# Moving two elementwise sums of a seven-product tile behind its first bank's reads, and computing six more tiles with seven products

## The chip, the cores and the metric

One core of a Trainium2 chip runs the whole program. The metric is the device time of one execution in microseconds (us). Three runs of the kernel before gave 838.73, 839.22 and 839.88 us, median 839.22 us. One further execution was profiled, and every duration below that carries a row or a place in time comes from it.

## The reference, cut to what matters

```
# x: (8, 3008, 256); w_r, w_i: (256, 256); moe_w_in: (256, 2048); moe_w_out: (2048, 256)
X  = rfft(x, axis=1)
Yr = Xr @ w_r - Xi @ w_i + b_r ;  Yi = Xr @ w_i + Xi @ w_r + b_i
Yr, Yi = soft_threshold(Yr, 0.01), soft_threshold(Yi, 0.01)
y  = irfft(Yr + 1j * Yi, n=3008, axis=1)              # (8, 3008, 256) -> 24064 rows of 256
h  = relu(y @ moe_w_in)                                # 2048 hidden values a row
out = (s * h * h + b) @ moe_w_out                      # 24064 rows of 256
```

The first half (spectral mixing, here "the attention part") is done batch by batch for eight batches. The second half (here "the expert part") takes the 24064 rows in tiles.

## The kernel before, in words

**Tiles and slots.** The rows are cut into 48 tiles, numbered here 0 to 47 in the order in which they are computed; most have 512 rows, some 480 or 384 (`_tile_order`, line 73). A tile takes 16 slots. In each slot `first_mm` (line 851) multiplies one block of 128 hidden units: two matmuls of 512 columns into a double bank `psh`. After every second slot ScalarE (ACT) applies the Relu to the pair (`rt`, line 871, three buffers) and VectorE (DVE) or ACT squares it into `gt` (lines 881 and 884). Which of the two squares is decided while the program is built: the planner adds each instruction's assumed cost to a running sum for each engine and takes the one that is free first (`act_first`, line 180). The second layer of tile t runs in the slots of tile t+1. "The window of tile t" below is that stretch, from the first matmul of tile t+1 to the first of tile t+2. The attention part of a later batch is mixed into the slots by a plan (`schedule`, line 1084). Its matmuls go through one of two `psf` banks, and its evacuations are again split between ACT and DVE. The order in which the instructions stand on each engine is finally set by a scheduling layer; `tc.issue_after(x)` keeps what is issued under it behind x.

**Two ways of doing the second layer.** An ordinary tile (`second_mms`, line 922) multiplies four blocks of 128 rows by 16 blocks of `w_out`: 64 matmuls of 256 columns, four a slot, and two evacuations `ost` (line 945). A tile "by seven products" (`seven_mms`, line 983) uses Strassen's scheme in Winograd's form: the activations and `w_out` are seen as two by two blocks, and seven products of half size take the place of eight. That is 112 matmuls of 128 columns, seven a slot. The right-hand sums (`T_s`) are made once. The left-hand sums are made for each tile and each half q of the hidden units (q is 0 or 1), by `s_op` (line 965), where A11, A12, A21, A22 are parts of `gt`:

- sum 1: s = A21 + A22, on DVE
- sum 3: A21 becomes A11 - A21, on DVE
- sum 2: A11 becomes A11 - s, on DVE, after product 0 has read A11
- sum 4: A12 becomes A12 + A11, as an accumulating DMA that GpSimd (POOL) issues (line 973), after product 1 has read A12

Products 0 and 1 use the old A11 and A12, product 2 uses A22, product 3 uses s, product 4 the new A11, product 5 the new A21, product 6 the new A12. Products 0 and 1 share one PSUM bank, product 2 has the next, products 3 and 4 share the one after, products 5 and 6 the last. In the first seven batches these banks come from the two `psa` buffers, so products 3 and 4 need the bank of products 0 and 1 back. `leave(0)` (line 1020) gives it back: DVE adds product 0 into `zz` (line 1028), product 1 into `ost` (line 1029), and makes a second copy of `zz` (line 1030). `leave(1)` to `leave(3)` take the other products out. In the last batch ("alone" in the code, tiles 41 to 45) the banks rotate over four buffers, and products 0, 1 and 2 are computed together.

**Which tiles, and when.** `seven(ti)` (line 1073) picks 21 tiles: 4 to 6, the two ahead of each batch's first tile from batch 2 on, the first tile of batches 3 to 6 ("late" tiles), and those of the last batch. Batch b's first tile is 12, 17, 23, 29, 35, 41 for b = 2 to 7. For q = 0, sums 1 and 3 are issued in slots 10 and 11 of the tile itself (for late tiles in slots 0 and 1 of its window). All others are issued in its window, at the slots that lines 1061 to 1067 list:

```
*first, (2, 2, 0), (2, 1, 1), (2, 4, 0), (3, 3, 1), (4, 2, 1), (5, 4, 1)     # (slot, sum, q)
...
(4 + alone, 0), (6, 1), (11, 2), (15, 3)                                     # (slot, leave)
```

Queues that matter here: DVE and ACT run their instructions in the order in which they stand. POOL issues the loads of `x` (line 234) and the accumulating DMAs in one order. SyncE (SP) issues the stores of the result and, shortly before a new batch, four loads `us<-ud` of 384 KB each (line 644), which all lie in the window of the tile two ahead of a batch's first.

Of the kernel before, what the change touches and what calls it, by code (L numbers as in the profile page):

```python
# [11 lines left out]
ALU = mybir.AluOpType  # L12
# [84 lines left out]
def kernel(  # L97
# [13 lines left out]
    nc = tc.nc  # L111
    B, S, D = x.shape
# [4 lines left out]
    MC = DFF // P  # L117
# [3 lines left out]
    first, fwd, inv, last = _tables(N)  # L121
# [50 lines left out]
    def matmul(out, lhs, rhs, **how):  # L172
        if pe["on"]:
            pe["now"] += 0.0025 + int(np.prod(rhs.shape[1:])) / 2400.0
        return nc.tensor.matmul(out, lhs, rhs, **how)  # L175

    def work(engine, us):
        load[engine] = max(load[engine], pe["now"]) + us
# [32 lines left out]
    def sum_bank(ti):  # L211
        return any_bank() if ti >= mark[B - 1] // MC else other_bank()
# [149 lines left out]
    b_21 = cpool.tile([P, P], F32, name="b_21")  # L362
# [3 lines left out]
    def w_block(k, j):  # L366
        return w_out_t.rearrange("p (q k) d -> p q k d", k=2)[:, :, k, j * P : (j + 1) * P]
# [447 lines left out]
    def sub_size(tl):  # L815
        return 4 * tl[3] if tl[0] == "wide" else P
# [13 lines left out]
    def halves(ti):  # L830
        return width(tiles[ti]) in (480, 512)
# [54 lines left out]
    def store(tl, sub, src):  # L886
        kind, b, j, w = tl
        if kind == "wide":
            h, lo = j
            n2 = HW * h + 4 * sub  # L890
            rows = out[b * N : (b + 1) * N, :].rearrange("(n1 n2) d -> n2 n1 d", n2=N2)
            nc.sync.dma_start(
                out=rows[n2 : n2 + 4, lo : lo + w], in_=src[0 : 4 * w]
            )
            return
        if kind == "main":
            rows = out[b * N + 512 * j : b * N + 512 * (j + 1), :]
            rows = rows.rearrange("(n1 n2) d -> n2 n1 d", n2=N2)[8 * sub : 8 * sub + 8]
            nc.sync.dma_start(out=rows, in_=src)
            return  # L900
        i0 = j + 128 * sub
        end = min(i0 + 128, j + w)
        i = i0
        while i < end:
            hb, r = divmod(i, N2 * 14)
            n2, n1 = divmod(r, 14)
            bt = 2 * b + hb
            rows = out[bt * N + 80 * N2 : (bt + 1) * N, :].rearrange(
                "(n1 n2) d -> n2 n1 d", n2=N2
            )  # L910
            room = min(end, (hb + 1) * N2 * 14) - i
            if n1 == 0 and room >= 14:
                m = room // 14
                cnt = 14 * m
                dst = rows[n2 : n2 + m]
            else:
                cnt = min(14 - n1, room)
                dst = rows[n2, n1 : n1 + cnt]
            nc.sync.dma_start(out=dst, in_=src[i - i0 : i - i0 + cnt])
            i += cnt  # L920
# [40 lines left out]
    def part(ti, q, i, k):  # L961
        size = 2 * sub_size(tiles[ti])
        return gts[(ti, q)][:, i, k, :, 0:size]

    def s_op(ti, n, q):

        size = 2 * sub_size(tiles[ti])
        if n == 1:
            sums[(ti, q)] = spool.tile([P, 4, 2 * P], F16, name="s1", tag="s1")
        s1 = sums[(ti, q)][:, :, 0:size]  # L970
        a11, a12, a21, a22 = (part(ti, q, i, k) for i in range(2) for k in range(2))
        if n == 4:
            nc.gpsimd.dma_start(out=a12, in_=a11, accum_op=ALU.add)  # L973
            return
        out, a, b, op = {
            1: (s1, a21, a22, ALU.add),
            3: (a21, a11, a21, ALU.subtract),
            2: (a11, a11, s1, ALU.subtract),
        }[n]
        nc.vector.tensor_tensor(out=out, in0=a, in1=b, op=op)  # L980
        work("dve", 0.07 + size / 480.0)

    def seven_mms(ti):

        tl = tiles[ti]
        size = sub_size(tl)
        hold = {}
        left = [(0, 0), (0, 1), (1, 1), None, (0, 0), (1, 0), (0, 1)]
        firsts = (0, 2, 3, 5)
        T = T_s[0]  # L990
        right = [w_block(0, 0), w_block(1, 0), T[:, 3], T[:, 0], T[:, 1], T[:, 2], w_block(1, 1)]

        def mm(n, j, c):

            if n in firsts and j == 0 and c == 0:
                hold["ps"] = sum_bank(ti).rearrange("p (n j e) -> p n j e", n=2, j=2)
            if j == 0 and c == 0:
                hold[n] = hold["ps"][0:size, 0 if n in firsts else 1]
            q, g = divmod(c, 4)
            at = slice(j * size, (j + 1) * size)  # L1000
            if left[n] is None:
                lhs = sums[(ti, q)][:, g, at]
            else:
                lhs = gts[(ti, q)][:, left[n][0], left[n][1], g, at]
            matmul(
                hold[n][:, j], lhs, right[n][:, c],
                start=(n in firsts and j == 0 and c == 0), stop=(c == MC // 2 - 1),
                skip_group_check=True,
            )

        def add(out, of, other):
            nc.vector.scalar_tensor_tensor(  # L1012
                out=out, in0=of, scalar=s_bc[0:size], in1=other, op0=ALU.mult, op1=ALU.add
            )
            work("dve", 0.4)

        def wide(t):
            return t[0:size, 0:P].unsqueeze(1).to_broadcast([size, 2, P])

        def leave(group):  # L1020
            if group == 0:
                hold["z"] = zpool.tile([P, 2, 2, P], F32, name="zz", tag="zz")
            if group in (0, 3):
                hold["o", group] = opool.tile([P, 2, D], F32, name="ost", tag="ost")
            z = hold["z"][0:size]
            top = hold["o", 0][0:size]
            if group == 0:
                add(z[:, 0], hold[0], wide(bias_bc))
                add(top[:, :, 0:P], hold[1], z[:, 0])
                nc.vector.tensor_tensor(out=z[:, 1], in0=z[:, 0], in1=wide(b_21), op=ALU.add)  # L1030
                work("dve", 0.34)
            elif group == 1:
                add(z[:, 0], hold[2], z[:, 0])
            elif group == 2:
                add(z[:, 1], hold[3], z[:, 1])
                two = hold[4].rearrange("p j e -> p (j e)").unsqueeze(1).to_broadcast([size, 2, D])
                zs = z.rearrange("p h j e -> p h (j e)")
                add(zs, two, zs)
                work("dve", 0.27)
            else:  # L1040
                for h in range(2):
                    add(hold["o", 3][0:size, :, h * P : (h + 1) * P], hold[5], z[:, h])
                add(top[:, :, P:D], hold[6], z[:, 1])
                for i in range(2):
                    for j in range(2):
                        store(tl, 2 * (1 - i) + j, hold["o", 3 * (1 - i)][:, j, :])

        C = MC // 2
        alone = ti >= mark[B - 1] // MC
        early = 3 if alone else 2  # L1050
        order = [
            (n, j, c) for h in range(2) for n in range(early) for j in range(2)
            for c in range(4 * h, 4 * h + 4)
        ]
        order += [(n, j, c) for n in range(early, 6) for j in range(2) for c in range(C)]
        order += [(6, j, c) for h in range(2) for j in range(2) for c in range(4 * h, 4 * h + 4)]
        slots = [[] for _ in range(MC)]
        for at, what in enumerate(order):
            slots[at // 7].append(lambda w=what: mm(*w))
        first = ((0, 1, 0), (1, 3, 0)) if late(ti) else ()  # L1060
        for at, n, q in (
            *first, (2, 2, 0), (2, 1, 1), (2, 4, 0), (3, 3, 1), (4, 2, 1), (5, 4, 1)
        ):
            at += alone and at > 3
            slots[at].append(lambda n=n, q=q: s_op(ti, n, q))
        for at, group in ((4 + alone, 0), (6, 1), (11, 2), (15, 3)):
            slots[at].append(lambda group=group: leave(group))
        return slots

    def late(ti):  # L1070
        return any(ti == mark[b] // MC for b in range(3, B - 1))

    def seven(ti):
        if ti >= len(tiles) - 2 or not halves(ti):
            return False
        firsts = [mark[b] // MC for b in range(2, B)]
        return (
            ti >= firsts[-1] or 4 <= ti < 7 or any(m - 2 <= ti < m for m in firsts)
            or late(ti)
        )  # L1080

# [19 lines left out]
    mark = {}  # L1101
# [76 lines left out]
```

## Time and profile before

| what | value |
|---|---|
| three runs | 838.73, 839.22, 839.88 us |
| the profiled execution | 839.64 us, of which the traced span is 837.9 us |
| granted TensorE clock | 0.996 |
| busy DVE, ACT, POOL | 706.9, 723.0, 86.2 us |
| Relu of a pair, 128x1024 | 1026 ns, 328 times |
| square of a pair on DVE / on ACT, 128x1024 | 1221 / 1061 ns |
| one sum on DVE, 128x1024 | about 687 ns |
| accumulating DMA, issue to landing | 3.3 to 8.8 us, median 4.5 us |

Matmuls are pipelined: a matmul's duration holds its way through the array, so the time that a matmul costs is read from the distance between starts, not from its duration. The same goes for DVE to a lesser degree: a 687 ns sum that follows an independent instruction starts 600 ns after it. A tile's window is found in the trace by the first `psh` matmul of each tile; tile 23's, for one, runs from 454.78 to 472.37 us.

### The profile page before, as it was taken

Reading aid. Unit: us, or ns where it says so; the run is one execution under the profiler, and the core shown is the slowest. Engines: PE = TensorE matmul, PEld = TensorE weight load, DVE = VectorE, ACT = ScalarE, POOL = GpSimd, SP = SyncE. Lnnn points to the kernel's source line nnn. Section 1 sums busy time; section 2 is a strip of 40 time slices with the busy share of each in tenths; the row PEclk is TensorE's granted clock in tenths of the full one; section 3 lists DMA queues with packets and bytes.
Section 4 is the critical chain, followed back from the end, with each engine's and each line's share of the span. In section 5 each row is a group of like instructions: output and inputs, shape, how many; then the busy total and the mean of one; then the engine's idle time right before and its main releaser. Section 6 shows DMA issues by size and latency. Waiting matters only on the chain.

```text
span 837.9 us, 19547 instructions
## 1 busy us (share of the span) xinstructions
PE 822.6 (98%) x7662; PEld 600.7 (72%) x7662; DVE 706.9 (84%) x1104; ACT 723.0 (86%) x962; POOL 86.2 (10%) x114
## 2 busy tenths in 40 slices
PE   8999999999999999999999999999999999999997
PEld 7857767777677767777677676767767777767765
DVE  5888989978898888988889888797889988889885
ACT  4998988998899989998889988989889988788882
POOL 4540001100011001100011000100001000001000
PEclk8999999999999999999999999999999999999999
DMA  8954578345873378444773368723565333513321
GB/s 196 180 153 103 124 189 203 63 94 133 198 185 65 94 184 208 114 104 128 195 185 69 88 147 208 175 63 105 127 178 138 67 100 93 137 45 77 72 65 60
DMA packets 116670, 107.17 MB, mean 128 GB/s; under 512 B 12774, under 2 KB 100842, under 8 KB 115234
## 3 DMA queue, kind: packets, MB, share of 16 engines
q1 hardware_dynamic: 102498, 80.55, 33.6%
q0 software_dynamic: 14080, 25.37, 19.1%
q8 instruction: 60, 0.98, 0.5%
q14 instruction: 32, 0.26, 0.1%
HBM read 53.52 MB, written 46.66 MB: 120 GB/s over the span
## 4 chain that ended last, share of the span: by engine, by line
PE 75%; DVE 12%; ACT 6%; DMA 3%; issue 3%; SPq 0%; POOL 0%; DVEq 0%; POOLq 0%
PE psh L175 31%; PE psa L175 28%; PE psf L175 16%; ACT rt L871 3%; DVE gt L884 2%; DVE gt L980 2%; ACT gt L881 1%; DVE ring L699 1%; PE psm L175 1%; DMA gt<-gt 1%; DVE ost L1012 1%; DMA ring<-ring 1%; DVE s L980 1%; DMA x<-in_x_dram 1%; DVE zz L1012 1%
## 5 line engine op out<-in xcount | busy, mean ns | idle before, releaser
L871 ACT ACTIVATE rt<-psh 128x1024 f32<-128x1024 f32 (+2 forms) x384 | 386.7, 1008 | 57.0 <-PE psh L175 55.1
L175 PEld LDWEIGHTS <-gt 128*128 128x128 f16 (+1 forms) x3696 | 304.8, 101 | 167.7 <-DMA gt<-gt 0.5
L175 PE MATMUL psh<-yt,w_in 128*128 128x512 f16 (+1 forms) x1344 | 397.1, 378 | 0.1
L884 DVE TENSOR_TENSOR gt<-rt 128x1024 f16<-128x1024 f32 (+2 forms) x239 | 286.2, 1202 | 78.6 <-ACT rt L871 77.6
L175 PE MATMUL psa<-w_out_t,gt 128*128 128x256 f16 (+3 forms) x2448 | 310.9, 253 | 0.3 <-DMA gt<-gt 0.3
L175 PEld LDWEIGHTS <-w_in 128*128 128x128 f16 x1536 | 136.5, 98 | 24.4 <-issue 1.7
L881 ACT ACTIVATE gt<-rt 128x1024 f16<-128x1024 f32 (+2 forms) x145 | 150.8, 1040 | 3.4
L175 PE MATMUL psa<-T_s,gt 128*128 128x128 f16 (+1 forms) x944 | 79.4, 219 | 0.0
L973 POOL DMA_DIRECT2D gt<-gt x42 | 38.0, 905 | 316.2 <-PE psh L175 66.3
L187 ACT CAST u<-psf 96x512 f16<-96x512 f32 x96 | 55.6, 581 | 9.3 <-PE psf L175 8.6
L699 DVE TENSOR_TENSOR ring<-psf,s 128x512 f16<-128x512 f32 x84 | 57.7, 686 | 3.5 <-PE psf L175 2.5
L187 ACT CAST v<-psf 128x512 f16<-128x512 f32 x79 | 45.8, 583 | 13.6 <-PE psf L175 13.5
L234 POOL DMA_DIRECT2D x<-in_x_dram x36 | 19.2, 539 | 325.1 <-PE psf L175 324.0
L175 PE MATMUL psh<-tail,w_in 128*128 128x512 f16 (+1 forms) x192 | 52.1, 353 | 0.0
L175 PEld LDWEIGHTS <-xf 128*128 128x128 f16 x504 | 46.6, 98 | 6.6 <-DVE xf L672 1.5
L175 PE MATMUL psf<-W_g,xf 128*128 128x256 f16 x336 | 50.4, 272 | 0.0
L187 ACT CAST yt<-psf 128x470 f16<-128x470 f32 (+2 forms) x84 | 43.3, 534 | 3.4 <-PE psf L175 2.2
L1012 DVE SCALAR_TENSOR_TENSOR ost<-psa,s_bc,zz 128x256 f32<-128x256 f32 (+1 forms) x80 | 35.9, 480 | 9.8 <-PE psa L175 8.2
L187 ACT CAST xf<-psf 128x512 f16<-128x512 f32 x64 | 37.4, 585 | 4.2 <-PE psf L175 3.9
L945 DVE SCALAR_TENSOR_TENSOR ost<-psa,s_bc,bias_bc 128x512 f32<-128x512 f32 (+2 forms) x51 | 37.1, 727 | 3.8 <-PE psa L175 1.4
L175 PE MATMUL psf<-x,A_t 94*96 94x512 f16 x102 | 39.0, 382 | 1.4 <-ACT yt L187 0.3
L175 PE MATMUL psf<-C_t,vs 96*128 96x94 f16 (+1 forms) x484 | 37.9, 205 | 0.0
(118 smaller groups left out, 802.6 us busy)
## 6 DMA issues: line engine op xcount, KB each, us to landing
out_dram<-ost SPq DMA_DIRECT2D x152, 128.0 KB
ud<-u SPq DMA_DIRECT2D x56, 192.0 KB
us<-ud SPq DMA_DIRECT2D x28, 384.0 KB
vd<-v SPq DMA_DIRECT2D x42, 256.0 KB
vs<-vd SPq DMA_DIRECT2D x14, 768.0 KB
x<-in_x_dram POOLq DMA_DIRECT2D x28, 376.0 KB, 6.0
gt<-gt POOLq DMA_DIRECT2D x38, 256.0 KB, 4.4
ring<-ring SPq DMA_DIRECT2D x280, 32.0 KB
```

Source lines behind the costliest of these rows:

```text
L175: return nc.tensor.matmul(out, lhs, rhs, **how)
L187: return None, nc.scalar.copy(out=dst, in_=src)
L234: nc.gpsimd.dma_start(out=t[0:N1, i * w : (i + 1) * w], in_=xv[:, c * XCH * D + i * w : c * XCH * D + (i + 1) * w],)
L699: nc.vector.tensor_tensor(out=ring[0][:, i % 4], in0=ps, in1=hold[i // 2][:, i % 2].unsqueeze(1).to_broadcast([P, 2, D]), op=ALU.add,)
L871: nc.scalar.activation(out=rt[:, :, 0:w], in_=ps[:, :, 0:w], func=AF.Relu)
L881: nc.scalar.activation(out=gt, in_=rr, func=AF.Square)
L884: last_square[0] = nc.vector.tensor_tensor(out=gt, in0=rr, in1=rr, op=ALU.mult)
L945: nc.vector.scalar_tensor_tensor(out=ost[0:size, 0:k], in0=ps[0:size, 0:k], scalar=s_bc[0:size], in1=bias_bc[0:size].unsqueeze(1).to_broad ...
L973: nc.gpsimd.dma_start(out=a12, in_=a11, accum_op=ALU.add)
L980: nc.vector.tensor_tensor(out=out, in0=a, in1=b, op=op)
L1012: nc.vector.scalar_tensor_tensor(out=out, in0=of, scalar=s_bc[0:size], in1=other, op0=ALU.mult, op1=ALU.add)
```

## The change

Sums 3 and 2 of half q = 1 now stand behind the third instruction of `leave(0)`; in the list, sum 1 of q = 1 moves from slot 2 to 3, sums 3 and 2 of q = 1 to slot 5, and `leave(0)` is put into its slot ahead of the sums. In the last batch all these are one slot later, as before. The choice of tiles widens from two to three ahead of a batch's first, which adds tiles 9, 14, 20, 26, 32 and 38 (27 tiles by seven products in place of 21). For these six, sum 4 of q = 1 is made by DVE, issued at slot 9, in place of the accumulating DMA.

```diff
+    def third_last(ti):
+        return any(ti == mark[b] // MC - 3 for b in range(2, B))
...
-        if n == 4:
+        if n == 4 and not (q == 1 and third_last(ti)):
             nc.gpsimd.dma_start(out=a12, in_=a11, accum_op=ALU.add)
             return
...
+            4: (a12, a12, a11, ALU.add),
...
-                nc.vector.tensor_tensor(out=z[:, 1], in0=z[:, 0], in1=wide(b_21), op=ALU.add)
+                hold["left"] = nc.vector.tensor_tensor(
+                    out=z[:, 1], in0=z[:, 0], in1=wide(b_21), op=ALU.add
+                )
...
+        def sums_behind(n, q, behind):
+            if behind:
+                with tc.issue_after(hold["left"].ins):
+                    s_op(ti, n, q)
+            else:
+                s_op(ti, n, q)
...
+        slots[4 + alone].append(lambda: leave(0))
         first = ((0, 1, 0), (1, 3, 0)) if late(ti) else ()
         for at, n, q in (
-            *first, (2, 2, 0), (2, 1, 1), (2, 4, 0), (3, 3, 1), (4, 2, 1), (5, 4, 1)
+            *first, (2, 2, 0), (2, 4, 0), (3, 1, 1), (5, 3, 1), (5, 2, 1),
+            (9 if third_last(ti) else 5, 4, 1),
         ):
-            at += alone and at > 3
-            slots[at].append(lambda n=n, q=q: s_op(ti, n, q))
-        for at, group in ((4 + alone, 0), (6, 1), (11, 2), (15, 3)):
+            at += alone and 3 < at < 8
+            slots[at].append(lambda n=n, q=q, at=at: sums_behind(n, q, at > 4 + alone))
+        for at, group in ((6, 1), (11, 2), (15, 3)):
             slots[at].append(lambda group=group: leave(group))
...
-            ti >= firsts[-1] or 4 <= ti < 7 or any(m - 2 <= ti < m for m in firsts)
+            ti >= firsts[-1] or 4 <= ti < 7 or any(m - 3 <= ti < m for m in firsts)
             or late(ti)
```

## The prediction

> **What bounds the kernel.** I read the page's first part, then the chain that ended last, the waits, and the timelines of the stretches that the change touches.
>
> ```profile
> PE 822.6 (98%) x7662; PEld 600.7 (72%) x7662; DVE 706.9 (84%) x1104; ACT 723.0 (86%) x962; POOL 86.2 (10%) x114
> ...
> PE 75%; DVE 12%; ACT 6%; DMA 3%; issue 3%; SPq 0%; POOL 0%; DVEq 0%; POOLq 0%
> ```
>
> TensorE is never idle for long. Busy time alone does not show that it is the bound, so I compare the distances between starts with the columns. In the timeline seven 128-column matmuls take 0.39 us (55.7 ns each), four 256-column ones 0.436 us (109 ns each). Summed that way over all 7662 matmuls, some 25 us of the span is not explained by columns, 9.5 of it in the first 47 us. From there on a matmul saved is time saved, and the places where it waits are few. The waits view names the largest of them:
>
> ```profile
> PE psa L175 <- DVE ost L1012: 4.5, 8, 0.9
> ...
> PEld L175 <- DVE ost L1012: 2.0, 6, 0.4
> ```
>
> This is product 3 waiting for the bank of products 0 and 1. One case, TensorE and then DVE (start, duration, what, count):
>
> ```profile
> 462.67 0.38 PE L175 MATMUL psf<-ring,T_t 128*128 128x256 f16 x2
> 462.89 0.38 PE L175 MATMUL psh<-yt,w_in 128*128 128x512 f16 x1
> 464.02 0.61 PE L175 MATMUL psa<-T_s,s 128*128 128x128 f16 x8 [0.75 <-DVE ost L1012]
> ```
>
> ```profile
> 460.48 0.69 DVE L980 TENSOR_TENSOR gt<-gt 128x1024 f16<-128x1024 f16 x1
> 461.08 0.69 DVE L715 TENSOR_TENSOR ring<-ring,high 128x1024 f16<-128x1024 f16 x1
> 461.69 0.69 DVE L980 TENSOR_TENSOR gt<-gt,s 128x1024 f16<-128x1024 f16 x1
> 462.29 0.69 DVE L716 TENSOR_TENSOR ring<-ring 128x1024 f16<-128x1024 f16 x1
> 462.89 0.48 DVE L1012 SCALAR_TENSOR_TENSOR zz<-psa,s_bc,bias_bc 128x256 f32<-128x256 f32 x1
> 463.28 0.29 DVE L672 TENSOR_TENSOR xf<-xf 128x256 f16<-128x256 f16 x1
> 463.48 0.49 DVE L1012 SCALAR_TENSOR_TENSOR ost<-psa,s_bc,zz 128x256 f32<-128x256 f32 x1
> ```
>
> A 512-column matmul takes 0.215 us, so product 3 could have started at 463.11; it started 0.91 late, when `ost` had ended. Ahead of `zz` stand two sums (L980). Measured alike, eleven windows wait: tiles 6, 17, 23, 29, 35 by 0.73, 0.92, 0.91, 1.07, 0.91 and tiles 4, 10, 21, 27, 33, 39 by 0.39, 0.31, 0.19, 0.43, 0.19, 0.44, together **6.5 us**. In the last batch the banks rotate and nothing waits.
>
> **Part 1: sums 3 and 2 behind `leave(0)`.** The built order confirms it: DVE meets `zz` and `ost` with those two sums behind them. Each sum costs DVE 0.60 (the distance of starts above), so `ost` ends up to 1.2 us earlier: at 462.7 in the case shown, ahead of 463.11. I take 6.2 of the 6.5 as won (bounds 4.5 and 6.5).
>
> What is late next is sum 4 of q = 1, the accumulating DMA. POOL starts it 0.64 after sum 2 ends (755.33 and 755.97), and product 6 needs it at its 105th matmul. In the new order sum 2 stands behind `leave(0)`, sum 3 and product 2's `zz`, which waits until product 2 is done, just when product 3 starts. So the DMA starts no earlier than 0.4 (`zz`) + 0.69 (sum 2) + 0.64, about 1.75 us, behind product 3. Today it is at about the same time as product 3:
>
> ```profile
> 428.45 0.87 POOL L973 DMA_DIRECT2D gt<-gt  x1 [2.51 <-DVE zz L1012]
> ...
> 755.97 0.86 POOL L973 DMA_DIRECT2D gt<-gt  x1 [2.40 <-DVE zz L1012]
> ```
>
> *Batches 1 to 6.* Late tiles keep their issue time, and those one ahead of a batch have 3.5 us or more to spare. In the windows two ahead of a batch, DMA time from issue and today's margin (until product 6 wants it) are: tile 4: 6.2, 1.5; 10: 6.7, 1.5; 15: 6.4, 2.6; 21: 8.8, none (it waits 0.44); 27: 7.0, 0.6; 33: 6.9, 1.6; 39: 3.3, 4.3. The issue moves by 1.2 to 2.7 us, and the lost bank waits bring product 6 nearer. If each landed as long after its issue as now, this adds 5.5 us. But those long landings are the four `us<-ud` loads sharing the DMA engines: a later issue meets less of them, and at tile 33, whose DMA already comes behind all four, nothing would change. I take 1.6 net: tile 4 0.1, tile 10 0.2, tile 21 0.5, tile 27 1.05 (its bank wait of 0.43 is gone too), 0.2 for the others, less the 0.44 of today; bounds 0 and 5.5.
>
> *Last batch.* There product 3 comes early and DVE is what lags:
>
> ```profile
> 748.83:761.99 13.16, 13.16 (x147) 9.38 (x145) 12.88 (x18) 10.68 (x11) 1.71 (x2) 1.00 0.33 71
> ...
> 406.26:421.69 15.43, 15.43 (x106) 10.32 (x105) 12.45 (x13) 11.79 (x17) 0.92 (x2) 1.00 0.82 208
> ```
>
> (length, then busy PE, PEld, DVE, ACT, POOL: DVE is busy 12.88 of 13.16.) In tile 41's window DVE reaches sum 2 of q = 0 at 751.39. By the new order there follow, at distances of starts from the rows, a square 1.13 (after 0.60), sum 1 0.60, a square 1.13, `zz` 0.40, a square 1.13, `ost` 0.40, `zz` 0.40, sum 3 0.60, `zz` 0.40: sum 2 starts at 758.2, not 754.64, and ends at 758.9. The DMA starts at 759.5, lands 3.3 later (as its two rows here do) at 762.8; product 6 wants it at 761.1. Cost 1.7. Part of it falls earlier, since product 4 wants the same sum 2 at 757. Tile 45's window is alike: 1.7. Between them the wait has taken away DVE's lag, so tile 42 costs 0 and tile 43 (landing 4.4 today, 0.1 late already) 0.7. Together **4.1 us** lost (bounds 1.5 and 6).
>
> **Part 2: six tiles by seven products.** 64 x 109 = 6.98 us becomes 112 x 55.7 = 6.24 us: 0.74 a tile, **4.4 us** (4.2 to 4.5). A rule speaks against it. The Trainium skill ("TensorE: Matmul & The Clock Gate", Back-to-back issue gap) gives a stream of weight load and matmul pairs about 81 ns a matmul at 128 columns and 131 at 512. By it 112 matmuls would take an estimated 9.1 us, and the six tiles would lose where the sum has them win; the trace disagrees, with 55.7 ns in 21 tiles.
>
> DVE gets seven sums and nine adds of `leave` a tile and loses two evacuations: 7 x 0.60 + 3.8 - 1.3 = 6.7 us. The built order shows 70 more DVE instructions and 14 more on ACT, so some 14 squares move over (2.3 a tile). DVE gains about 4.1 us a tile, ACT 2.3, over the tile and its window. In tile 20's window (406.26:421.69) 3.0 us of DVE and 3.6 of ACT are idle, in the stretch ahead about 2 each. It fits barely. Laid out by hand, `ost` of tile 20 ends 0.3 us after product 3 could start, and DVE enters the next window 2.3 us behind, which it makes good before product 3 there. I take 0.2 for each of six, 1.2 (0 to 3), and 0.5 for attention evacuations that come late on DVE (-0.3, since ACT may be free sooner, to 2). The six new accumulating DMAs (q = 0, issue at slot 2, wanted at slot 14) have 11 us and cost nothing. They stand on POOL ahead of an `x` load, which comes 1.8 us later anyway; were DVE later than that, the load would slip, with tens of us to spare. The six tiles' stores all come at the window's end, some 3 us ahead of the `us<-ud` loads behind them on SP. That costs nothing either; if it did, the loads and the DMA among them would shift together.
>
> **Sum.** 6.2 + 4.4 - 1.6 - 4.1 - 1.2 - 0.5 = 3.2 us off the profiled execution's 839.64 (span 837.9): 836.4. That execution is 0.42 above the runs' median, so **836.0 us**.
>
> **Rivals.**
> - *The DMAs have cover.* If the loads set the landing, and ACT takes the squares ahead of sum 2, the losses fall to 1.5 + 0 + 0.5: 10.6 - 2.0 = 8.6 off, 830.6. For it: the landing at tile 33. Against: DVE has no gap in the last batch. Chance 0.10.
> - *The accumulating DMA becomes the bound* (slower). Every landing keeps its length: 5.5 + 6, with 1.7 for the rest, against 10.6: 2.6 lost, 841.8. It decides from where the two DMA terms pass 8.9 us (5.7 taken). For it: it waits already at 437.34. Against: the loads are a fixed amount of work. With what else can be late on DVE, chance 0.25.
> - *Gains and new waits cancel*, DMA terms near 9: within 0.2%, 839. That is about what a measurement can tell from no change. Chance 0.21.
> - *Matmuls bound by weight loads in the six tiles.* The page has a weight load from `gt` at 98 ns. Were a 128-column matmul to wait for its own, 112 x 98 = 11.0 us would stand against 6.98: 4.0 lost in place of 0.74 won in each tile, 28 us more, 864. The 55.7 ns of 21 tiles with the same loads speak against it. Chance 0.01. (The rule above, from TensorE: Matmul & The Clock Gate in the Trainium skill, would be this rival's milder form.)
>
> The forecast holds 0.43. Faster by over 0.2% is 0.43 + 0.10 = 0.53, within 0.2% 0.21, slower 0.25 + 0.01 = 0.26. The range, 831 to 842, reaches to both rivals and leaves out a tenth at each end.
>
> **What would show it.** Right: product 3's waits for `ost` fall from 6.5 us to under 1.5; the windows of the six tiles shorten by about 0.5 to 0.7 us; tile 41's and 45's windows lengthen by about 1.7, with waits on sum 2 or on the accumulating DMA; more waits of TensorE for that DMA in windows two ahead of a batch. Wrong: no longer windows in the last batch (DVE's order cost nothing), or Relus waiting for `rt` in the six tiles' windows (DVE full), which I have at nothing.

## The result, and the profile after

The kernel after took 850.39, 851.82, 853.69 and 855.35 us, median **852.8 us**, beside 839.0 us for the kernel before on the same chip: a ratio of 1.016 (95% interval 1.013 to 1.0195; every ratio below is likewise to runs of the kernel before on the same chip). It is 13.7 us slower, where 3.2 us faster was predicted. The profiled execution is the slowest of the four, 855.35 us (span 853.6), so the traces are 15.7 us apart.

The page's first lines, and from the waits view those of TensorE (PE) and of its weight loads (PEld) for the names of the prediction (what waits, for what: us in total, times, longest us):

```profile
PE 822.0 (96%) x7950; PEld 598.1 (70%) x7950; DVE 724.1 (85%) x1174; ACT 737.9 (86%) x976; POOL 90.8 (11%) x120
```

```profile
PE psa L175 <- DMA gt<-gt: 8.2, 10, 1.6
PE psa L175 <- DVE ost L1016: 5.0, 12, 0.8
PE psf L175 <- DMA vs<-vd: 3.1, 4, 1.4
PE psf L175 <- DVE gt L984: 2.9, 4, 0.9
...
PEld L175 <- DVE ost L1016: 10.5, 21, 1.1
```

The waits for `ost` were to go; they have grown, and three kinds have come up that this view had at 0.5 us or less before: for the accumulating DMA `gt<-gt` (product 6), for sum 2 on DVE (`gt` L984, product 4) and for the load `vs<-vd`. PE's share falls from 98 to 96%, though it has fewer columns to do. (A wait counts under PE and under PEld where both stood, so these totals overlap. Below, a wait is what the distance between two matmul starts holds beyond the first one's columns.)

By that measure, profile after against profile before, in us:

| what | predicted | measured |
|---|---|---|
| columns | -4.4 | -4.4 |
| product 3's bank, the 21 old tiles | -6.2 | +0.8 (6.5 to 7.3) |
| product 3's bank, the six new windows | +1.2 | +1.9 |
| late accumulating DMA, batches 1 to 6 | +1.6 | +6.8 (0.4 to 7.2) |
| last batch | +4.1 | +6.1 |
| attention: evacuations, `vs` | +0.5 | +3.8 |
| attention, window of tile 2 (not the change, see below) | 0 | +1.3 |
| sum | -3.2 | +16.3 (-0.6 elsewhere makes 15.7) |

The columns are counted, not timed. The -0.6 holds 1.2 us by which the first `psh` matmul comes earlier in the profile after, in a stretch that the change does not touch: in the profile before, TensorE's granted clock was at half from 7.7 to 14.6 us, in the one after it was not.

Lengths of two windows, as shown of before: tile 20's (a new tile) and tile 41's (first of the last batch).

```profile
412.75:427.72 14.97, 14.87 (x154) 10.21 (x153) 14.23 (x21) 14.00 (x19) 1.81 (x3) 1.00 0.86 203
...
758.66:773.49 14.83, 13.51 (x146) 9.29 (x144) 13.54 (x19) 11.20 (x12) 1.71 (x2) 1.00 0.29 63
```

15.43 became 14.97 (0.46 shorter; 0.5 to 0.7 was forecast), and 13.16 became 14.83 (1.67 longer; 1.7 was forecast). DVE, with its seven sums and nine adds more, is now busy 14.23 of 14.97 us in the new tile's window. The whole gain there is 2.5 us in the six windows, and the windows that come next (tiles 10, 15, 21, 27, 33, 39) lengthen by 9.4 us together, 5.0 of them by late accumulating DMAs. Tile 21's, POOL and the wait of PE (the DMA goes out 10.62 us into the window, before 6.75, and lands 6.65 later):

```profile
438.34 0.86 POOL L976 DMA_DIRECT2D gt<-gt  x1 [4.85 <-PE psf L175]
```

```profile
445.04 0.23 PE L175 MATMUL psa<-w_out_t,gt 128*128 128x128 f16 x1 [1.02 <-DMA gt<-gt]
```

### The profile page after: what moved, and what is told of

It reads as the page before. It is cut to its first block, busy times and chain, and to the rows that moved or that the text cites. A ratio compares the mean times of both kernels' runs of the same rounds, so it can differ in the third digit from the quotient of the medians.

```text
span 853.6 us, 20228 instructions
## 1 busy us (share of the span) xinstructions
PE 822.0 (96%) x7950; PEld 598.1 (70%) x7950; DVE 724.1 (85%) x1174; ACT 737.9 (86%) x976; POOL 90.8 (11%) x120
## 5 line engine op out<-in xcount | busy, mean ns | idle before, releaser
L884 DVE TENSOR_TENSOR gt<-rt 128x1024 f16<-128x1024 f32 (+2 forms) x219 | 261.4, 1199 | 65.9 <-ACT rt L871 65.4
L175 PE MATMUL psa<-w_out_t,gt 128*128 128x128 f16 (+3 forms) x2352 | 279.2, 246 | 8.5 <-DMA gt<-gt 8.2
L881 ACT ACTIVATE gt<-rt 128x1024 f16<-128x1024 f32 (+2 forms) x165 | 172.3, 1044 | 3.5
L175 PE MATMUL psa<-T_s,gt 128*128 128x128 f16 (+1 forms) x1232 | 103.5, 219 | 0.0
L976 POOL DMA_DIRECT2D gt<-gt x48 | 43.2, 901 | 399.1 <-DVE s L984 78.0
L1016 DVE SCALAR_TENSOR_TENSOR ost<-psa,s_bc,zz 128x256 f32<-128x256 f32 (+1 forms) x104 | 46.8, 478 | 22.3 <-PE psa L175 19.3
L187 ACT CAST v<-psf 128x512 f16<-128x512 f32 x72 | 42.0, 583 | 13.1 <-PE psf L175 11.6
L175 PEld LDWEIGHTS <-s 128*128 128x128 f16 (+1 forms) x432 | 31.0, 100 | 24.8 <-DVE ost L1016 10.5
L1016 DVE SCALAR_TENSOR_TENSOR zz<-psa,s_bc,zz 128x256 f32<-128x256 f32 (+2 forms) x73 | 41.0, 562 | 0.9 <-PE psa L175 0.5
L984 DVE TENSOR_TENSOR gt<-gt 128x1024 f16<-128x1024 f16 (+1 forms) x60 | 41.0, 683 | 0.4
```

The source lines that it names most:

```text
L187: return None, nc.scalar.copy(out=dst, in_=src)
L881: nc.scalar.activation(out=gt, in_=rr, func=AF.Square)
L884: last_square[0] = nc.vector.tensor_tensor(out=gt, in0=rr, in1=rr, op=ALU.mult)
L1016: nc.vector.scalar_tensor_tensor(out=out, in0=of, scalar=s_bc[0:size], in1=other, op0=ALU.mult, op1=ALU.add)
```

## Product 3: the bank came earlier, and so did its reader

The late window of the prediction (tile 23's), PE and then DVE, in the kernel after:

```profile
469.47 0.50 PE L175 MATMUL psa<-T_s,gt 128*128 128x128 f16 x6
469.81 0.27 PE L175 MATMUL psf<-W_g,xf 128*128 128x256 f16 x1
470.74 0.23 PE L175 MATMUL psa<-T_s,s 128*128 128x128 f16 x1 [0.66 <-DVE ost L1016]
470.81 0.49 PE L175 MATMUL psf<-W_g,xf 128*128 128x256 f16 x3
```

```profile
469.21 0.48 DVE L1016 SCALAR_TENSOR_TENSOR zz<-psa,s_bc,bias_bc 128x256 f32<-128x256 f32 x1
469.61 0.68 DVE L716 TENSOR_TENSOR ring<-ring 128x1024 f16<-128x1024 f16 x1
470.20 0.48 DVE L1016 SCALAR_TENSOR_TENSOR ost<-psa,s_bc,zz 128x256 f32<-128x256 f32 x1
```

The window begins at 462.79, so `ost` starts 7.41 us into it, where before it started 8.70 into it: 1.28 earlier, as worked out. But before, product 3 stood behind four `W_g` matmuls, three of the first layer and two `T_t`. Now its first matmul stands behind one `W_g` matmul: the layer that orders the instructions has moved it ahead of 1.20 us of columns (8.32 us of columns stand before it in its window before, 7.12 after). The wait is 0.83 where it was 0.91.

In the windows of tiles 16, 22 and 34 a wait of 0.39 is new. Tile 22's, DVE, before (from 438.23) and after (from 445.93):

```profile
442.14 0.69 DVE L980 TENSOR_TENSOR s<-gt 128x1024 f16<-128x1024 f16 x1
442.75 0.29 DVE L672 TENSOR_TENSOR xf<-xf 128x256 f16<-128x256 f16 x1
442.95 0.69 DVE L980 TENSOR_TENSOR gt<-gt 128x1024 f16<-128x1024 f16 x1
443.55 0.48 DVE L1012 SCALAR_TENSOR_TENSOR zz<-psa,s_bc,bias_bc 128x256 f32<-128x256 f32 x1
443.94 0.69 DVE L980 TENSOR_TENSOR gt<-gt,s 128x1024 f16<-128x1024 f16 x1
444.54 0.48 DVE L1012 SCALAR_TENSOR_TENSOR ost<-psa,s_bc,zz 128x256 f32<-128x256 f32 x1
```

```profile
450.21 0.69 DVE L984 TENSOR_TENSOR s<-gt 128x1024 f16<-128x1024 f16 x1
450.93 1.23 DVE L884 TENSOR_TENSOR gt<-rt 128x1024 f16<-128x1024 f32 x1
452.07 0.48 DVE L1016 SCALAR_TENSOR_TENSOR zz<-psa,s_bc,bias_bc 128x256 f32<-128x256 f32 x1
```

Sum 3 is gone from ahead of `zz` and sum 2 from between `zz` and `ost`, and a square (L884) of 1.14 us stands ahead of both now. `zz` starts 6.14 into the window, where it was 5.32. Once the sums are issued later, the planner finds DVE free there and gives it the square (e4_order_old_split below tests this).

## Which part costs what

**e1_order and e2_tiles: each part alone.**

```diff
 # e1_order
-    return any(ti == mark[b] // MC - 3 for b in range(2, B))      # third_last
+    return False
-    ... any(m - 3 <= ti < m for m in firsts)
+    ... any(m - 2 <= ti < m for m in firsts)
 # e2_tiles: 27 tiles, the list of before, leave(0) behind the sums
-    *first, (2, 2, 0), (2, 4, 0), (3, 1, 1), (5, 3, 1), (5, 2, 1),
+    *first, (2, 2, 0), (2, 1, 1), (2, 4, 0), (3, 3, 1), (4, 2, 1),
```

> Part 1 alone: the sums moved, the 21 tiles of before. Theory A (both parts lose, each by its own mechanism): the order of the sums alone makes the accumulating DMA of q = 1 late in the windows two ahead of a batch, about 1 us in each of five and 1.6 in tile 4's, costs some 6 us in the last batch (tiles 41, 42, 43, 45 lengthen by 1.7, 1.2, 1.6, 1.6), and wins next to nothing at product 3: about 839 + 12 = 851 us. Theory B (the six new tiles' transfers make those DMAs late, and the order costs only the last batch and tile 4): 846 to 847 us. The prediction's own sum for this part: 838.5 us.

Measured: 851.2 us, ratio 1.015 (1.0125 to 1.017), 12.8 us above before. Theory A's number, and its parts in the main: product 6 waits for the DMA by 1.38, 1.35, 1.45 and 1.19 in the windows of tiles 4, 10, 21 and 27 (none in those of 15 and 33), product 3's waits are 5.6 of 6.5, and the last batch's four windows lengthen by 8.1, more than the 6 of the theory.

> Part 2 alone: 27 tiles by seven products, sums in the old order, sum 4 of q = 1 of the six new tiles by DVE at slot 9 as in the kernel after. Theory A: 4.4 us of columns won, 1.6 lost at the new windows' bank, some 4 lost to the load vs<-vd that now lands late behind the new accumulating DMAs: 840 to 842 us. Theory B (the same transfers also make the next window's accumulating DMA late, 5 us more): 845 us. The prediction's own sum: 836.3 us.

Measured: 845.6 us, ratio 1.008 (1.006 to 1.010), 7.3 us above before; theory B's number, but not its mechanism. Almost no DMA of q = 1 is late (product 6's waits are 0.2 in all). Product 3's are 14.9: 1.0 to 1.2 in five of the new windows and up to 1.15 in the windows that follow. So in the old order the new tiles lose at the bank, and the new order is what they need: four windows of 15.90 are 14.97 in the kernel after. The two parts' losses add to 20.1; together they cost 13.7.

**e3_tiles_dve: part 2 without its transfers.**

```diff
-        if n == 4 and not (q == 1 and third_last(ti)):
+        if n == 4 and not third_last(ti):
```

> As e2_tiles, with sum 4 of q = 0 of the six new tiles on DVE too, so that these tiles add no transfer. If the extra transfers crowd the DMA engines (theories A and B alike): PE's waits for vs<-vd at the start of the next window (0.6 to 1.6 us each) go, and the time is 836 to 838 us. Rival (DVE is what is full in these windows, and six more sums of 0.60 us push zz and the squares back): product 3 and the evacuations come later, and the time is that of e2_tiles or up to 4 us above it.

Measured: 844.7 us, ratio 1.0065 (1.004 to 1.009), within 1 us of e2_tiles. The rival holds: the waits for `vs` fall from 2.1 to 0.8, but product 3's are still 14.4, so without the transfers DVE's lag is nearly as dear.

**e4_order_old_split: part 1 alone, with before's choice of engine for every square and evacuation.**

```diff
-        return max(load["act"], ready) + ta <= max(load["dve"], ready) + td + lean[0]
+        return splits.pop(0) == "1"          # the kernel before's answers, in order
```

> As e1_order, but which engine takes each square and each evacuation is fixed to the choices of the kernel before (with the sums moved the planner gives DVE ten squares more). Theory C (the planner fills the time freed ahead of leave(0) with a square of 1.13 us, so that zz comes no earlier): product 3's waits that are new in tiles 16, 22 and 34's windows (0.39 each) go, and zz comes earlier elsewhere: 2 to 4 us below e1_order. Rival (the layer that orders the instructions puts other work there in any case, and ACT's squares come later instead): within 0.5 us of e1_order.

Measured: 846.6 us, ratio 1.009 (1.007 to 1.011), 4.6 us below e1_order. Theory C holds: `zz` of tile 22's window comes 4.89 us into it (before 5.32, e1_order 6.14), and its new wait is gone. Of the 4.6, product 3 gives 1.7 (5.6 to 3.9); the rest is sums 2 and DMAs that come earlier (product 4's waits fall by 1.2, product 6's by 1.7). Of product 3's 6.5 us before, 3.9 are left, all in the windows of tile 6 and the late tiles.

**e5_hold_p3: product 3 kept where it was.**

```diff
-            slots[at // 7].append(lambda w=what: mm(*w))
+            later = (late(ti) or ti == 6) and 48 <= at < 56
+            slots[8 if later else at // 7].append(lambda w=what: mm(*w))
...
+            if (late(ti) or ti == 6) and (n, j, c) == (3, 0, 0):
+                with tc.issue_after(hold_h["last"].ins):   # slot 8's first-layer matmul
+                    go()
```

> As e4_order_old_split, but in the windows of tiles 6, 17, 23, 29 and 35 the first matmul of product 3 is kept behind the first layer's matmuls of slot 8, where the kernel before has it within one matmul. Theory D (ost does come 1.2 us earlier there, but the layer that orders the instructions moved product 3 forward by the same 1.2 us of columns, and so kept the wait): the waits of 0.8 us go, the five windows shorten by 0.6 to 0.9 each, 3 to 4 us below e4_order_old_split, 843 us. Rival (DVE ends ost no earlier, or the wait returns at the next product or at a bank of psh): within 1 us of e4_order_old_split.

Measured: 844.3 us, ratio 1.006 (1.0046 to 1.008), some 2.5 below e4_order_old_split, and in the profile no wait for the bank is left in any window. Tile 23's window (455.66 to 472.36), PE, and its line by windows:

```profile
463.77 0.59 PE L176 MATMUL psh<-yt,w_in 128*128 128x512 f16 x2
464.20 1.00 PE L176 MATMUL psa<-T_s,s 128*128 128x128 f16 x15
```

```profile
455.66:472.36 16.70, 16.70 (x188) 12.64 (x186) 15.25 (x30) 16.13 (x20) 1.71 (x2) 1.00 0.42 90
```

PE is busy 16.70 of 16.70, and the window is 0.88 shorter than before. Theory D holds: the 0.9 us of a late window could be had, by moving the sums *and* keeping the reader of the bank in its place. The total fell by less than the four windows' 3.3: in this execution tile 4's product 6 waited 1.5 longer, the windows of tiles 18 and 24 gave back 0.45 each, and in tile 6's window, the fifth, product 6 took over half of what product 3 no longer waited.

**e11_last_batch: the new order in the last batch alone** (the old list elsewhere, 21 tiles).

```diff
+    def behind_it(ti):
+        return ti >= mark[B - 1] // MC       # new list and leave(0) ahead only there
```

> The kernel before, with the new order only in the last batch (tiles 41, 42, 43, 45). Theory: product 4's waits for sum 2 (3.6 us) and product 6's for the DMA (2.6 to 4.6 us) are all of it, and nothing is won: 6 to 8 us above before, 845 to 847 us. The prediction's sum: 4.1 us, 843 us.

Measured: 847.4 us, ratio 1.010 (1.009 to 1.0115), 8.5 us above before; the four windows lengthen by 2.2, 2.1, 1.6 and 2.0, product 4's waits are 3.6 and product 6's 4.4, as the theory has it. The prediction's 4.1 was half of it. (The kernel after, with the same order, lost 6.1 there: its DMAs of q = 1 landed 3.2 to 3.3 us after their issue, here 3.2 to 4.1. Sum 1 of q = 1 stays in slot 3 in the last batch, not one slot later.) In the kernel after, tile 41's window, POOL and the two waits on PE:

```profile
769.25 0.86 POOL L976 DMA_DIRECT2D gt<-gt  x1 [5.86 <-DVE s L984]
```

```profile
768.68 0.84 PE L175 MATMUL psf<-T_s,gt 128*128 128x128 f16 x12 [0.88 <-DVE gt L984]
772.60 0.23 PE L175 MATMUL psa<-w_out_t,gt 128*128 128x128 f16 x1 [0.44 <-DMA gt<-gt]
```

Product 4 waits for sum 2, which starts 9.29 us into the window (worked out: 9.4; before: 5.82). The DMA goes out 10.59 in (worked out: 10.7) and lands 3.3 later, and product 6 waits again.

**e6_q1_dve: no accumulating DMA of q = 1 in the kernel after.**

```diff
-        if n == 4 and not (q == 1 and third_last(ti)):
+        if n == 4 and q == 0:
-            (9 if third_last(ti) else 5, 4, 1),
+            (9, 4, 1),
```

> The kernel after with sum 4 of q = 1 on DVE at slot 9 in every tile by seven products, so that no accumulating DMA of q = 1 is left. Theory E (product 6 waits because of the DMA's 1.3 us of issue and 3.3 to 7 us of transfer): its waits (7.8 us in batches 1 to 6, 2.6 in the last batch) go, at 21 sums of 0.60 us on a DVE that has some room behind leave(0); product 4's waits for sum 2 (3.6 us in the last batch) stay: 843 us, bounds 841 to 846. Rival (the sum itself is late on DVE, behind sums 3 and 2 and the squares, and pushes the squares back): 849 us or more.

Measured: 846.2 us, ratio 1.008 (1.0065 to 1.010), 6 to 7 us below the kernel after. Product 6's waits for the DMA, 7.2 us and 2.6 in the last batch, are gone; product 4's 3.6 stay. Theory E's mechanism holds, though the time is 3 us above its middle and just outside its bounds: product 3's waits rose from 9.2 to 10.7, and the windows of tiles 16, 22 and 34, ahead of which DVE now has the sum, lengthened by 0.8 each.

**e8_q0_dve: the kernel after, without the new tiles' transfers** (the edit of e3_tiles_dve).

> The kernel after with sum 4 of q = 0 of the six new tiles on DVE, so that these tiles add no transfer. Crowding theory: PE's waits for vs<-vd (4.0 us) fall below 1.5, and the DMAs of q = 1 in the next windows land earlier: 848 to 850 us. Rival (DVE is what is full, as e3_tiles_dve beside e2_tiles suggests: 1 us between them): 851 to 853 us.

Measured: 855.0 us, ratio 1.018 (1.015 to 1.0205): not the crowding theory's 848 to 850, and above the rival's 851 to 853. In the profiled execution the granted clock fell to half for 3.4 us twice, from 146.6 and from 252.4 us, where matmuls stand twice as far apart; that is 3.3 us, without which it would be 852.0. The other three executions have mean clocks of 0.994 to 0.997 as well, three of the kernel after's four 1.000. So the rival holds. The waits for `vs` fall from 4.0 to 1.9, and four new windows go to 14.70 us (no wait at all); but product 6 still waits for the DMAs (7.8 us where it was 7.2; 2.9 of it in tile 10's window, where it was 1.3).

**e13_transfers_alone and e15_transfers_placed: the transfers without new tiles.** In these an accumulating DMA from `gt` into a spare buffer is added to the kernel before; nothing is left out.

```diff
+                if mc == 3 and ti - 1 in (9, 20, 26, 32):            # e15
+                    t = spool.tile([P, 4, 2 * P], F16, name="s1", tag="s1")
+                    with tc.issue_after(hold_h["last"].ins):
+                        nc.vector.memset(t, 0.0)
+                    nc.gpsimd.dma_start(out=t, in_=part(ti - 1, 0, 0, 0), accum_op=ALU.add)
```

> The kernel before, and in the windows of tiles 9, 14, 20, 26 and 32 an accumulating DMA of the same size, queue and slot as the new tiles' (slot 2, from gt), into a buffer that nothing reads (cleared by POOL before); no new tile by seven products. If the transfers alone make vs<-vd late: waits of 0.4 to 1.6 us at the start of windows 11, 22 and 28 (none in the seven profiles without new tiles), 2 to 4 us above before. Rival (DVE's extra work makes it late): within 0.7 us of before and no such waits.

> The kernel before with an accumulating DMA of the new tiles' size in the windows of tiles 9, 20, 26 and 32, behind the first layer's slot 3 (its target cleared there by DVE, 0.3 us) and ahead of the same load of x as in the kernel after; no new tile. If the transfers alone make vs<-vd late: PE waits of 0.3 to 1.6 us for vs<-vd in the windows of tiles 10, 21 and 27, 1 to 3 us above before. Rival (DVE's fuller queue is needed for it): no such wait above 0.3 us, within 0.7 us of before.

(The first counts windows 11, 22 and 28 by the tile whose first layer fills them: they are the windows of tiles 10, 21 and 27.) Measured: 840.9 us, ratio 1.001 (0.9996 to 1.003), and 840.3 us, ratio 1.001 (0.9998 to 1.002). Both are inconclusive: in both profiles the DMA of tiles 9, 20 and 26 went out some 6 us *before* its window began, where the new tiles have it 3.9 us *into* theirs. In the window of tile 10 `vs` is waited for even so (2.1 and 1.7 us; 0 in the profile of before), in those of tiles 21 and 27 it is not. But in these two profiles `vs` itself is issued 12.8 and 12.2 us into the window of tile 9, where before and the kernel after have it at 7.0 and 7.2, so this is not what delays it in the kernel after. More telling is e8_q0_dve: without the new transfer the load is issued at 7.0 as before and is not waited for in tile 10's window; with it, issued 0.2 later, it is waited for by 1.55. The five kernels with that transfer wait there by 0.25 to 1.8, the three that have the new tile without it by 0 to 0.3. In that one window the transfer delays the landing. How the rest of the kernel after's 4.0 us is shared between crowded DMA engines and a fuller DVE stays open; the 0.9 in tile 15's window needs no new tile (1.1 in e4_order_old_split).

## Is there something to win?

**e7_mixed**: new order, with sum 4 of q = 1 on DVE, in tiles 9, 20, 26, 32 and in those two ahead of a batch.

```diff
-        return any(ti == mark[b] // MC - 3 for b in range(2, B))
+        return ti in (9, 20, 26, 32)
+    def behind_it(ti):                   # new list here, sum 4 of q = 1 on DVE
+        return third_last(ti) or any(ti == mark[b] // MC - 2 for b in range(2, B))
```

> The new order only where its cost is not met: in four new tiles (9, 20, 26, 32; not 14 and 38) and in the tiles two ahead of a batch, all of them with sum 4 of q = 1 on DVE at slot 9; old order in the other tiles, the last batch among them. If the costs are those found so far (late DMAs, the last batch, psf<-ring,T_t after tile 14): the four windows win 0.46 each as in the kernel after, the windows two ahead some 0.2 each, the rest as before: 836 to 838 us. Rival (any sum more on DVE in these windows comes back as a later product 3 or vs<-vd): 840 us or more.

Measured: 843.1 us, ratio 1.004 (1.003 to 1.006): the rival. The four windows won 0.46 each; the windows of tiles 16, 22 and 34 lost 0.9, 1.05 and 0.9 (PE waits for `psf<-W_t,xf`, late on DVE), tile 10's 1.3.

**e10_new_tiles_own_order**: part 2, with the new order in the new tiles only (`behind_it` is `third_last`).

> Part 2 with the new order in the six new tiles only; all others in the old order. Theory F (part 2's loss is in the bank wait of the new windows, 1.2 us each in the old order, and in what follows them): the six windows go back to 14.97 from 15.90 us, 5.3 us below e2_tiles, 840 us. Rival (the new tiles are late on DVE in either order, and what is won in their windows is lost in the next): 843 to 846 us.

Measured: 842.5 us, ratio 1.003 (1.002 to 1.005), 3.6 us above before: 4.0 us better than e2_tiles by the two ratios, not the 5.3 of theory F. The windows did go to 14.98, but those of tiles 10, 21, 27, 33 and 39 still lengthened by 1.6, 0.4, 0.55, 0.9 and 0.5, and tile 13's by 0.9 (tile 15's by 0.6, as in e1_order without new tiles).

**e9_late_hold**: the kernel before, with the new order and the held product 3 in the four late tiles only (`behind_it` is `late`). **e12_four_more**: the same, the new order also in tiles 16, 22, 34, 39, and the split of before.

> The kernel before, with the new order only in the four late tiles (17, 23, 29, 35) and the first matmul of product 3 kept behind slot 8's first-layer matmuls there. Theory D: those four windows go from 17.6 to 16.7 us as in e5_hold_p3, and the following windows give 0.45 back twice (psf<-x,A_t): 3.6 - 0.9 = 2.7 us below before, a ratio of 0.997. Rival (the next windows take back all of it, or DVE's later sums come due somewhere else): within 1 us of before.

> As e9_late_hold, with the new order also in tiles 16, 22, 34 and 39, whose windows were shorter than before in e4_order_old_split (by 0.15, 0.10, 0.15 and 0.42), and the squares and evacuations split as in the kernel before. If windows add up: 0.8 us below e9_late_hold, 3.5 us below before. Rival (what a window wins the next one gives back, as each starts with DVE later): the same as e9_late_hold.

Measured: 836.7 us, ratio 0.998 (0.9966 to 0.999), and **835.2 us, ratio 0.9962 (0.9949 to 0.9975)**: 3.7 us faster than the kernel before by the medians, and the best of all kernels here. The late windows are 16.7 us in both (tile 29's 16.9). The windows of tiles 16, 22, 34 and 39 are shorter by 0.15, 0.10, 0.25 and 0.42 in e12_four_more: what those windows win is kept in the trace, though the two intervals overlap and the fixed split is a second difference between the two kernels.

**e14_four_new_tiles**: e12_four_more, and tiles 9, 20, 26, 32 by seven products, both sums 4 on DVE, the planner free.

> e12_four_more, and tiles 9, 20, 26 and 32 by seven products in the new order with both sums 4 on DVE (no new transfer); the planner free. The four windows go from 15.43 to 14.70 us as in e8_q0_dve (2.9 us won). Theory (DVE enters the next window late, product 3 waits there for 0.3 to 1.1 us as in e10): 1.5 to 2.5 us lost again, so 0.4 to 1.4 us below e12_four_more. Rival (the planner's other choices for squares cost more than that): 1 us or more above e12_four_more.

Measured: 836.9 us, ratio 0.9975 (0.9956 to 0.9994), not told apart from e12_four_more. The four windows win 0.73 each, 2.9 us, all that the columns promise; the four that follow lose 0.6, 0.95, 0.3 and 0.95, nearly as much, and those of tiles 16, 22, 34 another 0.4 each. These last are product 3's 0.39 of e1_order again, where the free planner put a square ahead of `zz`. So part 2 paid nothing in any kernel here; new tiles with a fixed split were not tried.

## Why the prediction was wrong, step by step

- **"`ost` ends up to 1.2 us earlier ... I take 6.2 of the 6.5 as won."** This step failed, and with 7 us of the 19 between forecast and measured trace it is the largest: product 3's waits went from 6.5 to 7.3 in the same 21 tiles. Clearing DVE's queue was only half of what it took. In the late windows the bank was free 1.28 us earlier, and product 3, which I had kept at its old place on PE, was moved forward by 1.20 us of columns (e5 shows the missing half). In the windows of tiles 16, 22 and 34 the freed place went to a square (e4 against e1), and `zz` came later. The step looked only at the two sums in DVE's built order, not at what else had moved there and on PE.
- **"I take 1.6 net" for the DMAs two ahead of a batch.** Failed in size: 6.8, above the upper bound of 5.5. Two things were wrong. Most of it came without the new tiles: in e1_order the issue moved by 2.2 to 2.7 us in four windows, as worked out or nearly, and product 6 waited 5.4, about the 5.5 of landings that keep their length; the cover hoped for was missing. With the new tiles the issue moved by up to 4.6: in the window of tile 21 the DMA went out 10.6 us into it, where it was 6.75, because a planner's square and the lag from the new tile stood ahead of sum 2. That later issues meet less traffic did show at two places (windows of tiles 15 and 33 in e1_order: landing after 3.4 and 4.0 us where it was 6.4 and 6.9), but not at tiles 4, 10, 21 and 27 (5.9 to 7.3). "Late tiles keep their issue time" was wrong too (10.65 us into three of the windows, where it was 8.2), but cost nothing: product 6 does not wait there.
- **The last batch, 4.1.** Tile 41's window was right (1.7 predicted, 1.67 measured; sum 2 and the DMA within 0.1 us), tile 45's too (1.7 and 1.61). DVE's order was worked out well; that the total fits is partly luck, since it hangs on a landing of 3.3 us: in e1_order and e11_last_batch the DMA of tile 41 went out at the same place, landed after 3.9 and 3.8, and the window lengthened by 2.2. "Between them the wait has taken away DVE's lag, so tile 42 costs 0 and tile 43 0.7" failed: 1.20 and 1.64. In tile 42's window DVE stands idle from 3.8 to 4.5 us for the Relu of its next square, two squares stand ahead of sum 2, and that comes 8.91 us in, where it had come 5.37 before.
- **Part 2's columns, 4.4**, right to a tenth: where nothing waits, a new tile's window is 0.73 shorter (e8_q0_dve, e14_four_new_tiles; 0.74 forecast). **The new windows' bank, 1.2:** 1.9 measured. The 14 squares that were to move to ACT were 20 (239 to 219 on DVE), and the sign given for a full DVE, Relus waiting for `rt`, did not show.
- **"The six new accumulating DMAs ... cost nothing"; 0.5 for attention.** Failed: 3.8. In the windows that follow a new tile, PE waits for `vs<-vd`, 4.0 in all, which no term had (0.9 of it, tile 15's, comes without new tiles too), and the window in which new tile 14's first sums are made has 0.9 more of `psf<-ring,T_t`. In the window of tile 20 the DMA engines' share rises from 0.82 to 0.86, the `x` load goes out 0.7 us later, and the two loads of `vs` are issued 0.7 later as well. Which of these decides there is not settled; in tile 10's window it is the landing.
- **"DVE enters the next window 2.3 us behind, which it makes good before product 3 there"** failed too: in the windows of tiles 21 and 33 product 3 waits 0.5 us in the kernel after (0.2 before), and 1.1 in e10 and e14.
- The rivals: "the accumulating DMA becomes the bound" had the right side (841.8) and much of the mechanism, with a fifth of the loss. Its two DMA terms, 11.5, measured 12.9 (3.6 of them product 4's waits for sum 2), but it left the gains at 10.6 us, and only the 4.4 came.

## What to carry to other kernels

When a wait is to be shortened by moving the work ahead of it, look at both ends in the built order: an ordering layer that sees the bank free earlier may bring the reader forward by as much, and a planner may fill the freed place. Pin the reader where it was, then take the work away. And where an engine is busy 80 to 95% of a window, price added work in the *next* windows: here the 0.46 or 0.73 us won in each of four new tiles' windows were followed by 0.3 to 1.6 us lost in the window after it (e10, e14).

## What the runs showed of the hardware

The same instructions take different times where DMA traffic ends a wait. In the window of tile 4, e1_order, the kernel after and e8_q0_dve have the same DVE order, and PE waited for the accumulating DMA by 1.38, 1.77 and 2.15 us; e4_order_old_split and e5_hold_p3 are alike there too, and waited 1.22 and 2.69 (landing 7.2 and 8.7 us after issue). In the window of tile 2 the kernel before has no wait for `psf<-ring,T_t` and e9_late_hold, alike up to there, has 1.0 us of it. That is why the 1.3 us there are not put down to the change; it may also be why the kernel after's runs spread over 5 us, which one profile cannot show. The same 256 KB transfer landed 3.2 to 8.8 us after its issue over the kernels before and after, and 3.2 to 5.2 in the last batch, where no `us<-ud` loads run.

In e8_q0_dve the granted clock fell to half for 3.4 us twice, 0.6 and 0.9 us after the end of TensorE's two longest waits for the DMA (2.15 and 2.94 us), and each time some 1.7 us was lost on top of the wait. After the 2.69 us of e5_hold_p3 it did not fall, so these runs show no length of wait from which it falls, nor that the wait is the cause.
